# A gate's division by remainder with all its intermediates in SBUF, and its denominator scaled on ScalarE

## Chip, cores and metric

The kernel runs on one core of a Trainium2 chip. The metric is device time in microseconds (us). TensorE (PE) multiplies matrices, VectorE (DVE), ScalarE (ACT) and GpSimd (POOL) work element by element, and SyncE (SP) issues the DMAs. SBUF is the working memory on the core, PSUM holds what PE writes.

## What is computed

Sliding-window attention of 8 batches and 8 heads over 576 positions, and behind it a feed-forward layer of 4608 tokens, 512 to 2048 to 512, whose activation is a rational function:

```python
scores = scale * np.matmul(q, k.transpose(0, 1, 3, 2))     # masked to a window of 64
attn = np.exp(scores - np.max(scores, axis=-1, keepdims=True))
attn = attn / (np.sum(attn, axis=-1, keepdims=True) + 1e-09)
x = np.matmul(attn, v)                                      # heads joined: 4608 x 512
h = x @ w_in
P = a[0] + a[1] * h + a[2] * h**2 + a[3] * h**3
Q = 1.0 + np.abs(b[0]) * np.abs(h) + np.abs(b[1]) * h**2
out = (P / (Q + 1e-6)) @ w_out
```

The weights come as 64-bit floats and are decoded on the chip.

## The kernel before

**Tiling.** The tokens go in 12 chunks of 384 (CH). The inner width of 2048 goes in 16 slices of 128. One *step* is one slice of one chunk: `ffn1` (line 234) makes h, 128 x 384, by 12 matmuls into PSUM and issues the gate; `ffn2` (line 270) multiplies the gate's result with w_out, 9 matmuls into three accumulators of 128 x 512. There are 192 steps. Every matrix operand is split into a high part, rounded to PE's fp32r format, and a low part, the remainder; so each product is three matmuls (high with high, low with high, high with low), and each gate must deliver gh (high) and gl (low).

**Attention.** A chunk has four attention units (two heads each). A unit loads q, k and v, makes scores on PE (S in ps_s, line 182), scales and masks them on DVE (lines 188 and 192), takes the maximum (nmx, line 198), runs six exponentials on ACT that also sum (line 201), adds and inverts the sums on DVE (203, 204), scales on POOL (sm, line 205), transposes on PE (212), copies on ACT (pT, 214), and multiplies with v (223), from which ACT and DVE make xh and xl (228, 229). A unit comes about every four steps.

**Decoding.** `decode` (line 101) loads a slice of 512 columns, makes the 32-bit number in five DVE instructions (lines 113 to 118), rounds it on ACT (121) and subtracts on POOL (122). There are 32 decodes, spread over the first 20 or so steps.

**The gate** (lines 241 to 261), step by step: ACT takes ah = |h| (244) and num = a3 h + a2 (245), both from PSUM; DVE makes num = (num h) and then (num + a1) h (246, 247); POOL makes u = b1 ah + b0 (248) and u = u ah (249), so that Q = u + QADD with QADD = 1 + 1e-6; ACT takes ah = Ln(u + QADD) (251) and ah = Exp(-ah) (252), a first value of 1/Q; DVE refines it by one Newton step, u = (u + QADD) ah and u = (2 - u) ah (253, 254), and makes num = (num + a0) u (255); ACT rounds it to gh (258), and gl = num - gh (260) runs on POOL for the first 20 gates (GLN) and on DVE for the rest.

**Order and buffers.** Every engine takes its instructions in program order and waits at each for what it needs. That order is made by a scheduler at build time, which simulates the engines, so that an edit of the gate can move other instructions too. The tiles ah, u and num have two buffers each (pool tmp), gh and gl four (LAG + 1), h two, each accumulator one. So a step's tiles come free when the second step before it is done with them. `ffn2` of a step is written three steps (LAG) after its `ffn1`.

Of the kernel before, what the change touches and what calls it, by code (L numbers as in the profile page):

```python
# [9 lines left out]
F32 = mybir.dt.float32  # L10
F32R = mybir.dt.float32r
U32 = mybir.dt.uint32
AF = mybir.ActivationFunctionType
ALU = mybir.AluOpType
# [3 lines left out]
CH = 384  # L18
TC = CH // WIN
PR = TC // 2  # L20
GLN = 20
AHEAD = 3
LAG = 3
W_AT = 0, 1, 2, 3
# [3 lines left out]
QADD = 1.0 + 1e-6  # L28
# [3 lines left out]
def swa_rational_ffn(ctx: ExitStack, tc: tile.TileContext, qT, kT, v, w_in, w_out, a, b, out):  # L32
    nc = tc.nc
    P = 128
# [17 lines left out]
    gp = ctx.enter_context(tc.tile_pool(name="gp", bufs=LAG + 1))  # L52
    op = ctx.enter_context(tc.tile_pool(name="op", bufs=2))
# [26 lines left out]
    a_sb = const.tile([P, 4], F32, name="a_sb")  # L80
    b_raw = const.tile([P, 2], F32, name="b_raw")
    b_sb = const.tile([P, 2], F32, name="b_sb")
# [146 lines left out]
        nc.vector.tensor_tensor(out=xl[c, hp], in0=x, in1=xh[c, hp].bitcast(F32), op=ALU.subtract)  # L229

    gs = {}
    n_gates = [0]

    def ffn1(c, i):
        h = ps_h.tile([P, CH], F32, name="h")
        n = 0
        for cc in range(NCC):
            for w, x in ((wi_h, xl), (wi_h, xh), (wi_l, xh)):
                nc.tensor.matmul(h, w[:, cc, i * P:(i + 1) * P], x[c, cc], start=n == 0, stop=n == 3 * NCC - 1)  # L239
                n += 1  # L240
        ah = tmp.tile([P, CH], F32, name="ah")
        u = tmp.tile([P, CH], F32, name="u")
        num = tmp.tile([P, CH], F32, name="num")
        nc.scalar.activation(ah, h, AF.Abs)  # L244
        nc.scalar.activation(num, h, AF.Identity, scale=a_sb[:, 3:4], bias=a_sb[:, 2:3])  # L245
        nc.vector.tensor_tensor(out=num, in0=num, in1=h, op=ALU.mult)
        nc.vector.scalar_tensor_tensor(out=num, in0=num, scalar=a_sb[:, 1:2], in1=h, op0=ALU.add, op1=ALU.mult)  # L247
        nc.gpsimd.tensor_scalar(out=u, in0=ah, scalar1=b_sb[:, 1:2], scalar2=b_sb[:, 0:1], op0=ALU.mult, op1=ALU.add)  # L248
        nc.gpsimd.tensor_tensor(out=u, in0=u, in1=ah, op=ALU.mult)  # L249

        nc.scalar.activation(ah, u, AF.Ln, bias=QADD)  # L251
        nc.scalar.activation(ah, ah, AF.Exp, scale=-1.0)  # L252
        nc.vector.scalar_tensor_tensor(out=u, in0=u, scalar=QADD, in1=ah, op0=ALU.add, op1=ALU.mult)  # L253
        nc.vector.scalar_tensor_tensor(out=u, in0=u, scalar=2.0, in1=ah, op0=ALU.subtract, op1=ALU.mult, reverse0=True)  # L254
        nc.vector.scalar_tensor_tensor(out=num, in0=num, scalar=a_sb[:, 0:1], in1=u, op0=ALU.add, op1=ALU.mult)  # L255
        gh = gp.tile([P, CH], F32R, name="gh")
        gl = gp.tile([P, CH], F32R, name="gl")
        nc.scalar.copy(out=gh, in_=num)  # L258
        n_gates[0] += 1
        (nc.gpsimd if n_gates[0] <= GLN else nc.vector).tensor_tensor(out=gl, in0=num, in1=gh.bitcast(F32), op=ALU.subtract)  # L260
        gs[c, i] = gh, gl


# [83 lines left out]
    for s in range(total + LAG):  # L347
        for fn, *args in todo.get(s, ()):
            if fn in (load_w_in, load_w_out):
                fn(*args)  # L350
        if s < total:
            ffn1(*steps[s])
        for fn, *args in todo.get(s, ()):
            if fn not in (load_w_in, load_w_out):
                fn(*args)
        if s >= LAG:
            ffn2(s - LAG)
# [31 lines left out]
```

## Time and profile before

| | |
|---|---|
| median of 3 runs | 1064.74 us (1063.88 to 1066.21) |
| the profiled execution, its span | 1063.77 us, 1062.0 us |
| PE busy | 963.7 us, 91% of the span, 6624 matmuls |
| DVE busy | 917.7 us, 86%, 1583 instructions |
| ACT busy | 674.3 us, 63%, 1702 |
| POOL busy | 525.0 us, 49%, 511 |

How to read the profile: it is one execution, with times from its start. A group's row gives line, engine, operation, output and inputs, shape, count, then the busy time in us, the mean of one in ns, and the idle time of its engine just before, with what ended it. A row in the order of time begins with its start and its duration. A row of waits says who waited for whom: us in total, times, longest. A row of a stage gives its limits and length, then the busy time and count of PE, its weight load, DVE, ACT and POOL, and then PE's granted clock, the DMA's share and GB/s. A line's own row gives the least, the median and the greatest duration in ns. PE's matmuls overlap, so its busy time is no measure of its throughput. L260 is line 260.

### The profile page before, as it was taken

What the parts mean: (1) busy time and instruction counts of PE and PEld (TensorE: products, weight loads), DVE (VectorE), ACT (ScalarE), POOL (GpSimd) and SP (SyncE); (2) the same over time, 40 slices, a digit from 0 to 9 for tenths busy, and PEclk for the clock granted to TensorE, in tenths of its full rate; (3) what the DMA queues carried; (4) which work ended last, traced back from release to release, by engine and by line L of the source; (5) the groups of instructions that cost most, each with busy time, mean ns of one, the idle gap of its engine ahead of it and who ended that gap; (6) DMA issues with size and microseconds to landing.
All of it is one profiled execution on the core that took longest, in us unless ns stands there. A gap on an engine that the chain in (4) does not pass through costs nothing.

```text
span 1062.0 us, 18218 instructions
## 1 busy us (share of the span) xinstructions
PE 963.7 (91%) x6624; PEld 846.0 (80%) x6624; DVE 917.7 (86%) x1583; ACT 674.3 (63%) x1702; POOL 525.0 (49%) x511
## 2 busy tenths in 40 slices
PE   2558667899999999999999999999999999999997
PEld 2446555778888888888888888888888888888996
DVE  6999989988888898898888888888888888888885
ACT  3454445467666766766766766766666667667654
POOL 5356658864454445435435535534444444454432
PEclk9778779899999999999999999999999999999999
DMA  5543343102121121110211211210211211200000
GB/s 183 173 152 93 107 130 110 35 1 73 48 66 30 59 58 32 63 61 28 70 45 29 69 48 33 92 31 28 85 29 30 88 30 32 93 16 1 31 2 30
DMA packets 68538, 64.10 MB, mean 60 GB/s; under 512 B 4448, under 2 KB 61792, under 8 KB 68448
## 3 DMA queue, kind: packets, MB, share of 16 engines
q1 hardware_dynamic: 68448, 62.93, 19.0%
q8 instruction: 52, 0.85, 0.3%
q14 instruction: 38, 0.31, 0.1%
HBM read 53.48 MB, written 9.44 MB: 59 GB/s over the span
## 4 chain that ended last, share of the span: by engine, by line
DVE 36%; ACT 20%; POOL 19%; PE 17%; issue 5%; DMA 3%; POOLq 0%; SPq 0%; DVEq 0%; ACTq 0%
PE o L280 8%; ACT sm L201 8%; POOL u L248 7%; PE h L239 7%; DVE u L253 7%; POOL u L249 6%; POOL sm L205 4%; DVE u L254 4%; DVE nmx L198 4%; DVE num L255 2%; ACT ah L251 2%; DVE w_c L117 2%; DVE gl L260 2%; ACT ah L252 2%; DVE w_c L118 2%
## 5 line engine op out<-in xcount | busy, mean ns | idle before, releaser
L239 PE MATMUL h<-xl,wi_h 128*128 128x384 f32 x768 | 269.4, 351 | 30.3 <-DVE num L247 22.3
L248 POOL TENSOR_SCALAR u<-ah,b_sb 128x384 f32<-128x384 f32 x192 | 164.6, 860 | 262.8 <-ACT ah L244 199.6
L239 PE MATMUL h<-xh,wi_h 128*128 128x384 f32 x768 | 264.3, 344 | 0.0
L239 PE MATMUL h<-xh,wi_l 128*128 128x384 f32 x768 | 263.5, 343 | 0.0
L280 PE MATMUL o<-wo_h,gl 128*128 128x512 f32 x576 | 236.8, 411 | 25.4 <-DVE gl L260 14.4
L280 PE MATMUL o<-wo_h,gh 128*128 128x512 f32 x576 | 228.6, 397 | 0.0
L280 PE MATMUL o<-wo_l,gh 128*128 128x512 f32 x576 | 228.0, 396 | 0.0
L249 POOL TENSOR_TENSOR u<-u,ah 128x384 f32<-128x384 f32 x192 | 204.5, 1071 | 9.8
L239 PEld LDWEIGHTS h<-xl,wi_h 128*128 128x128 f32 x768 | 148.2, 193 | 40.1 <-DVE num L247 26.1
L205 POOL TENSOR_TENSOR sm<-sm,rs 128x768 f32<-128x768 f32 x48 | 81.4, 1696 | 195.8 <-DVE rs L204 195.8
L201 ACT ACTIVATE sm<-sm,nmx 128x128 f32<-128x128 f32 x288 | 111.9, 390 | 102.7 <-DVE nmx L198 102.4
L260 DVE TENSOR_TENSOR gl<-num,gh 128x384 fp32r<-128x384 f32 x172 | 154.0, 899 | 13.0 <-ACT gh L258 10.0
L245 ACT ACTIVATE num<-h,a_sb 128x384 f32<-128x384 f32 x192 | 128.5, 670 | 45.7 <-DVE gl L260 35.8
L280 PEld LDWEIGHTS o<-wo_h,gl 128*128 128x128 f32 x576 | 109.6, 190 | 58.9 <-DVE gl L260 19.2
L239 PEld LDWEIGHTS h<-xh,wi_h 128*128 128x128 f32 x768 | 148.5, 193 | 4.7
L253 DVE SCALAR_TENSOR_TENSOR u<-u,ah 128x384 f32<-128x384 f32 x192 | 116.7, 608 | 40.9 <-ACT ah L252 39.2
L251 ACT ACTIVATE ah<-u 128x384 f32<-128x384 f32 x192 | 100.4, 523 | 80.2 <-POOL u L249 79.3
L239 PEld LDWEIGHTS h<-xh,wi_l 128*128 128x128 f32 x768 | 148.3, 193 | 0.0
L280 PEld LDWEIGHTS o<-wo_h,gh 128*128 128x128 f32 x576 | 109.7, 190 | 25.2
L258 ACT CAST gh<-num 128x384 fp32r<-128x384 f32 x192 | 96.7, 508 | 47.5 <-DVE num L255 47.4
L280 PEld LDWEIGHTS o<-wo_l,gh 128*128 128x128 f32 x576 | 109.9, 191 | 18.7
L255 DVE SCALAR_TENSOR_TENSOR num<-num,a_sb,u 128x384 f32<-128x384 f32 x192 | 121.1, 636 | 2.9
(45 smaller groups left out, 1274.1 us busy)
## 6 DMA issues: line engine op xcount, KB each, us to landing
out<-ob SPq DMA_DIRECT2D x33, 256.0 KB, 2.0
w_st<-w_in SPq DMA_DIRECT2D x16, 512.0 KB, 3.7
w_st<-w_out SPq DMA_DIRECT2D x16, 512.0 KB, 3.6
q<-qT SPq DMA_DIRECT2D x32, 192.0 KB, 3.4
vt<-v SPq DMA_DIRECT2D x16, 384.0 KB, 3.4
vt<-v SPq DMA_DIRECT2D x16, 320.0 KB, 3.3
kt<-kT SPq DMA_DIRECT2D x16, 224.0 KB, 3.5
kt<-kT SPq DMA_DIRECT2D x16, 192.0 KB, 3.5
```

Of the source, the lines that this page charges most:

```text
L201: nc.scalar.activation(sm[:, j, :], sm[:, j, :], AF.Exp, bias=nmx[:, j:j + 1], accum_out=sums[:, j:j + 1])
L205: nc.gpsimd.tensor_tensor(out=sm, in0=sm, in1=rs.unsqueeze(2).broadcast_to([P, NR, P]), op=ALU.mult)
L239: nc.tensor.matmul(h, w[:, cc, i * P:(i + 1) * P], x[c, cc], start=n == 0, stop=n == 3 * NCC - 1)
L245: nc.scalar.activation(num, h, AF.Identity, scale=a_sb[:, 3:4], bias=a_sb[:, 2:3])
L248: nc.gpsimd.tensor_scalar(out=u, in0=ah, scalar1=b_sb[:, 1:2], scalar2=b_sb[:, 0:1], op0=ALU.mult, op1=ALU.add)
L249: nc.gpsimd.tensor_tensor(out=u, in0=u, in1=ah, op=ALU.mult)
L251: nc.scalar.activation(ah, u, AF.Ln, bias=QADD)
L253: nc.vector.scalar_tensor_tensor(out=u, in0=u, scalar=QADD, in1=ah, op0=ALU.add, op1=ALU.mult)
L255: nc.vector.scalar_tensor_tensor(out=num, in0=num, scalar=a_sb[:, 0:1], in1=u, op0=ALU.add, op1=ALU.mult)
L258: nc.scalar.copy(out=gh, in_=num)
L260: (nc.gpsimd if n_gates[0] <= GLN else nc.vector).tensor_tensor(out=gl, in0=num, in1=gh.bitcast(F32), op=ALU.subtract)
L280: nc.tensor.matmul(acc[c][t], g[:, ts], w[:, i, :], start=first and n == 0, stop=last and n == 2)
```

## The change

The gate divides in another way. The product of num + a0 and the first value of 1/Q is rounded to fp32r as it is written, and that is gh. Then the remainder of the division is formed, num + a0 - (u + QADD) gh, and multiplied with the same value of 1/Q; that is gl. The Newton step, the rounding copy on ACT and the subtraction for gl go. The scaling b1 ah + b0 goes from POOL to ACT. POOL keeps the product u ah, and no gl runs on POOL any more.

```diff
-        nc.gpsimd.tensor_scalar(out=u, in0=ah, scalar1=b_sb[:, 1:2], scalar2=b_sb[:, 0:1], op0=ALU.mult, op1=ALU.add)
+        nc.scalar.activation(u, ah, AF.Identity, scale=b_sb[:, 1:2], bias=b_sb[:, 0:1])
...
         nc.scalar.activation(ah, u, AF.Ln, bias=QADD)
         nc.scalar.activation(ah, ah, AF.Exp, scale=-1.0)
-        nc.vector.scalar_tensor_tensor(out=u, in0=u, scalar=QADD, in1=ah, op0=ALU.add, op1=ALU.mult)
-        nc.vector.scalar_tensor_tensor(out=u, in0=u, scalar=2.0, in1=ah, op0=ALU.subtract, op1=ALU.mult, reverse0=True)
-        nc.vector.scalar_tensor_tensor(out=num, in0=num, scalar=a_sb[:, 0:1], in1=u, op0=ALU.add, op1=ALU.mult)
-        nc.scalar.copy(out=gh, in_=num)
-        n_gates[0] += 1
-        (nc.gpsimd if n_gates[0] <= GLN else nc.vector).tensor_tensor(out=gl, in0=num, in1=gh.bitcast(F32), op=ALU.subtract)
+        nc.vector.scalar_tensor_tensor(out=gh, in0=num, scalar=a_sb[:, 0:1], in1=ah, op0=ALU.add, op1=ALU.mult)
+        nc.vector.scalar_tensor_tensor(out=u, in0=u, scalar=QADD, in1=gh.bitcast(F32), op0=ALU.add, op1=ALU.mult)
+        nc.vector.scalar_tensor_tensor(out=num, in0=num, scalar=a_sb[:, 0:1], in1=u, op0=ALU.add, op1=ALU.subtract)
+        nc.vector.tensor_tensor(out=gl, in0=num, in1=ah, op=ALU.mult)
```

In the changed kernel the lines are: 246 scaling on ACT, 247 and 248 num, 249 the product on POOL, 252 Ln, 253 Exp, 254 gh, 255 and 256 the remainder, 257 gl; the attention's lines are smaller by one, the output's by three.

Where the instructions stand. First ACT around the softmax of one attention unit in the middle of the program, before (each row is an instruction, its output and inputs and their size):

```order
L251 ACTIVATE ah<-u 128x384
L228 CAST xh_5434<-ps_x 128x384
L252 ACTIVATE ah<-ah 128x384
L251 ACTIVATE ah<-u 128x384
L252 ACTIVATE ah<-ah 128x384
L201 ACTIVATE sm,sums<-sm,nmx 128x128 x6
L258 CAST gh<-num 128x384
L244 ACTIVATE ah<-h 128x384
L258 CAST gh<-num 128x384
L245 ACTIVATE num<-h,a_sb 128x384
```

The same place on ACT now:

```order
L252 ACTIVATE ah<-u 128x384
L227 CAST xh_4917<-ps_x 128x384
L253 ACTIVATE ah<-ah 128x384
L252 ACTIVATE ah<-u 128x384
L253 ACTIVATE ah<-ah 128x384
L200 ACTIVATE sm,sums<-sm,nmx 128x128 x6
L244 ACTIVATE ah<-h 128x384
L245 ACTIVATE num<-h,a_sb 128x384
L246 ACTIVATE u<-ah,b_sb 128x384
```

The two copies to gh behind the six exponentials are gone, and each step has the scaling (L246) behind num. In the one unit of four that ends a chunk, one copy of the output (ob) now stands behind the exponentials, and two ahead of them.

Next DVE at the same kind of place, before:

```order
L253 SCALAR_TENSOR_TENSOR u<-u,ah 128x384
L188 SCALAR_TENSOR_TENSOR sm<-ps_s,mask 128x384 x2
L253 SCALAR_TENSOR_TENSOR u<-u,ah 128x384
L254 SCALAR_TENSOR_TENSOR u<-u,ah 128x384
L198 TENSOR_REDUCE nmx<-sm 128x6
L254 SCALAR_TENSOR_TENSOR u<-u,ah 128x384
L255 SCALAR_TENSOR_TENSOR num<-num,a_sb,u 128x384 x2
L203 TENSOR_SCALAR sums<-sums 128x6
L204 RECIPROCAL rs<-sums 128x6
L260 TENSOR_TENSOR gl<-num,gh 128x384 x2
```

And now:

```order
L187 SCALAR_TENSOR_TENSOR sm<-ps_s,mask 128x384 x2
L254 SCALAR_TENSOR_TENSOR gh<-num,a_sb,ah 128x384 x2
L197 TENSOR_REDUCE nmx<-sm 128x6
L255 SCALAR_TENSOR_TENSOR u<-u,gh 128x384 x2
L256 SCALAR_TENSOR_TENSOR num<-num,a_sb,u 128x384 x2
L257 TENSOR_TENSOR gl<-num,ah 128x384 x2
L202 TENSOR_SCALAR sums<-sums 128x6
L203 RECIPROCAL rs<-sums 128x6
```

The two gl have moved ahead of the instruction on the softmax's sums; in some units the second of them stands between it and the reciprocal.

Last POOL in the startup, while weights are decoded, before:

```order
L248 TENSOR_SCALAR u<-ah,b_sb 128x384
L205 TENSOR_TENSOR sm<-sm,rs 128x768
L260 TENSOR_TENSOR gl<-num,gh 128x384 x2
L122 TENSOR_TENSOR wo_l<-w_c,wo_h 128x512
L249 TENSOR_TENSOR u<-u,ah 128x384
L122 TENSOR_TENSOR wo_l<-w_c,wo_h 128x512
L260 TENSOR_TENSOR gl<-num,gh 128x384
L122 TENSOR_TENSOR wo_l<-w_c,wo_h 128x512
L260 TENSOR_TENSOR gl<-num,gh 128x384
L122 TENSOR_TENSOR wo_l<-w_c,wo_h 128x512
```

And now:

```order
L249 TENSOR_TENSOR u<-u,ah 128x384
L121 TENSOR_TENSOR wo_l<-w_c,wo_h 128x512
L249 TENSOR_TENSOR u<-u,ah 128x384
L204 TENSOR_TENSOR sm<-sm,rs 128x768
L121 TENSOR_TENSOR wo_l<-w_c,wo_h 128x512
L121 TENSOR_TENSOR wi_l<-w_c,wi_h 128x4x128
```

L248 and L260 are gone from POOL. On DVE, 17 gl now stand ahead of the last instruction of the last decode, where none stood; there were 16 whole gates ahead of it and now there are 17. PE's order has the same groups, and differs in the startup, at the ends of chunks and at the end, where the products of three steps follow the last h, and before it of four.

More of the change, by code (lines that the diff above doesn't have):

```diff
@@ L20 @@
 PR = TC // 2
-GLN = 20
 AHEAD = 3
@@ L231, in swa_rational_ffn @@
     gs = {}
-    n_gates = [0]
     def ffn1(c, i):
@@ L243, in ffn1 @@
         num = tmp.tile([P, CH], F32, name="num")
+        gh = gp.tile([P, CH], F32R, name="gh")
+        gl = gp.tile([P, CH], F32R, name="gl")
         nc.scalar.activation(ah, h, AF.Abs)
         nc.scalar.activation(num, h, AF.Identity, scale=a_sb[:, 3:4], bias=a_sb[:, 2:3])
+        nc.scalar.activation(u, ah, AF.Identity, scale=b_sb[:, 1:2], bias=b_sb[:, 0:1])
         nc.vector.tensor_tensor(out=num, in0=num, in1=h, op=ALU.mult)
         nc.vector.scalar_tensor_tensor(out=num, in0=num, scalar=a_sb[:, 1:2], in1=h, op0=ALU.add, op1=ALU.mult)
-        nc.gpsimd.tensor_scalar(out=u, in0=ah, scalar1=b_sb[:, 1:2], scalar2=b_sb[:, 0:1], op0=ALU.mult, op1=ALU.add)
         nc.gpsimd.tensor_tensor(out=u, in0=u, in1=ah, op=ALU.mult)
@@ L252, in ffn1 @@
         nc.scalar.activation(ah, ah, AF.Exp, scale=-1.0)
[L253 to L258, printed above, removed]
-        n_gates[0] += 1
-        (nc.gpsimd if n_gates[0] <= GLN else nc.vector).tensor_tensor(out=gl, in0=num, in1=gh.bitcast(F32), op=ALU.subtract)
+        nc.vector.scalar_tensor_tensor(out=gh, in0=num, scalar=a_sb[:, 0:1], in1=ah, op0=ALU.add, op1=ALU.mult)
+        nc.vector.scalar_tensor_tensor(out=u, in0=u, scalar=QADD, in1=gh.bitcast(F32), op0=ALU.add, op1=ALU.mult)
+        nc.vector.scalar_tensor_tensor(out=num, in0=num, scalar=a_sb[:, 0:1], in1=u, op0=ALU.add, op1=ALU.subtract)
+        nc.vector.tensor_tensor(out=gl, in0=num, in1=ah, op=ALU.mult)
         gs[c, i] = gh, gl
```

## The prediction

> **What bounds the kernel now.** I read the page's slices first, then the stages, then who waits for whom in each. The slices (each digit tenths of a slice of 26.6 us):
>
> ```profile
> PE   2558667899999999999999999999999999999997
> DVE  6999989988888898898888888888888888888885
> ```
>
> TensorE (PE) is filled only from the eighth slice on; before that VectorE (DVE) is the full engine. The busy times by stage (microseconds; columns PE, weight load, DVE, ACT, POOL) put figures to it:
>
> ```profile
> 58.00:205.00 147.00, 100.53 (x609) 83.97 (x608) 139.46 (x219) 73.86 (x188) 101.18 (x77) 0.81 0.35 106
> 300.00:940.00 640.00, 628.28 (x4474) 557.82 (x4473) 551.39 (x979) 442.80 (x1138) 299.84 (x294) 1.00 0.16 49
> ```
>
> So there are two regimes. From 58 to 205 us the weights are decoded while the first gates run: DVE is busy 139.5 of 147 us, PE idles 46.5, and a microsecond less on DVE is about one less in the end. From 300 to 940 us PE idles only 640 - 628.3 = 11.7 us, and only that can be won. The waits of PE in that stretch have a single row, and its largest part looks like this in the order of time (start, duration, what, idle before):
>
> ```profile
> PE o L280 <- DVE gl L260: 11.7, 9, 1.6
> ...
> 456.80 0.40 ACT L201 ACTIVATE sm<-sm,nmx 128x128 f32<-128x128 f32 x1 [2.77 <-DVE nmx L198]
> ...
> 459.50 0.91 ACT L258 CAST gh<-num 128x384 fp32r<-128x384 f32 x2
> ...
> 457.15 1.14 DVE L255 SCALAR_TENSOR_TENSOR num<-num,a_sb,u 128x384 f32<-128x384 f32 x2
> ...
> 460.03 2.48 DVE L260 TENSOR_TENSOR gl<-num,gh 128x384 fp32r<-128x384 f32 x2 [0.38 <-ACT gh L258]
> ...
> 459.11 0.33 PE L239 MATMUL h<-xh,wi_l 128*128 128x384 f32 x1
> 460.82 0.50 PE L280 MATMUL o<-wo_h,gl 128*128 128x512 f32 x1 [1.38 <-DVE gl L260]
> ```
>
> The gate's values num are complete at 457.15 + 1.14 = 458.3, but their rounded copy gh stands on ACT behind six softmax exponentials that wait for nmx, so gl starts at 460.03 and PE loses 1.38 us.
>
> **The change, steady stage.** gh is now written by DVE itself from num and the exponential, and gl follows two DVE instructions later; no step of the gate after Exp leaves DVE, and in the new order both gl stand ahead of the softmax sums that DVE awaits from ACT, or one of them does. Counted with the durations above, the four instructions take the place of u, u, num, gl one for one, so the first gl would end near 458.3 + 0.55 = 458.9, ahead of the 459.4 at which PE's last h matmul ends. What is late next is the front of the chain. The scaling u, now on ACT, waits behind num instead of running on POOL beside it. No row shows this instruction; the nearest are
>
> ```profile
> L251 ACT ACTIVATE ah<-u 128x384 f32<-128x384 f32 x192 | 100.4, 523 | 80.2 <-POOL u L249 79.3
> ...
> L245 ACT ACTIVATE num<-h,a_sb 128x384 f32<-128x384 f32 x192 | 128.5, 670 | 45.7 <-DVE gl L260 35.8
> ...
> L258 ACT CAST gh<-num 128x384 fp32r<-128x384 f32 x192 | 96.7, 508 | 47.5 <-DVE num L255 47.4
> ...
> L248 POOL TENSOR_SCALAR u<-ah,b_sb x192: 654/688/2607, 58.5 to 1048.2; 128x384 f32<-128x384 f32 x192
> ...
> 338.66 2.44 ACT sm L201 x12
> 357.83 2.44 ACT sm L201 x12
> ```
>
> (The last row but two gives the least, the median and the most in ns; the last two are the softmax of two attention units in the chain that ended last.) The two ends are 0.52 us (SBUF source, no scale operand) and 0.67 us (two operands per partition, PSUM source). I take 0.70, since it has both the operands and the SBUF source. ACT gains 0.70 and loses 0.51 a step, 0.19 x 130 steps = 25 us in the 640, so 468 of 640 us: not a bound. The chain to Exp gets longer by about num's 0.57 (start to start) plus 0.70 less POOL's 0.69, 0.6 us, and shorter behind it by the copy's 0.51 and by the wait for ACT. Laid out for one attention unit (four steps, 357.83 - 338.66 = 19.2 us) with these durations I find the first gl of the unit about 1.3 us ahead of PE's need; before it is 0.35 us ahead in an ordinary unit:
>
> ```profile
> 439.21 0.56 DVE L260 TENSOR_TENSOR gl<-num,gh 128x384 fp32r<-128x384 f32 x1
> ...
> 440.12 0.39 PE L280 MATMUL o<-wo_h,gl 128*128 128x512 f32 x1
> ```
>
> (439.77 against PE's turn to it at 440.12). One wait is added: ah is now read until gl, so Abs of step s waits for gl of step s-2; behind it in ACT's queue stand num, the scaling, Ln and Exp of the step, and POOL and DVE wait for those. Before, num waited for that same gl, so Abs alone moves, by some 0.4 us. gh's buffer is asked for earlier too, but there are four of them and the second product of step s-4 precedes the end of h of step s in PE's order. So all nine waits go: **-11.7 us**; the ends are -11.7 and, if each only moves to another instruction, 0.
>
> **The change, startup.** Here DVE is the bound, and it shares something with POOL. A stretch without POOL's work beside it gives the bare durations, the groups of the stage (us busy, mean ns) the real ones:
>
> ```profile
> 90.09 0.55 DVE L253 SCALAR_TENSOR_TENSOR u<-u,ah 128x384 f32<-128x384 f32 x1
> 90.56 0.41 DVE L113 TENSOR_SCALAR w_c<-w_st 128x512 uint32<-128x512 uint32 x1
> 90.90 0.68 DVE L117 SCALAR_TENSOR_TENSOR w_c<-w_st,w_c 128x512 uint32<-128x512 uint32 x1
> ...
> 92.91 0.60 DVE L255 SCALAR_TENSOR_TENSOR num<-num,a_sb,u 128x384 f32<-128x384 f32 x1
> ...
> L118 DVE SCALAR_TENSOR_TENSOR w_c<-w_st,w_c 128x512 uint32<-128x512 uint32 x31 | 31.9, 1034 | 0.1
> L117 DVE SCALAR_TENSOR_TENSOR w_c<-w_st,w_c 128x512 uint32<-128x512 uint32 x32 | 30.6, 959 | 0.3
> L114 DVE TENSOR_SCALAR w_c<-w_c 128x512 f32<-128x512 f32 x32 | 20.8, 648 | 0.3
> L116 DVE TENSOR_SCALAR w_c<-w_c 128x512 uint32<-128x512 uint32 x32 | 19.9, 621 | 0.3
> L113 DVE TENSOR_SCALAR w_c<-w_st 128x512 uint32<-128x512 uint32 x32 | 18.4, 574 | 16.7 <-DMA w_st<-w_in 12.7 <-DMA w_st<-w_out 1.5 <-POOL wo_l L122 1.4
> L253 DVE SCALAR_TENSOR_TENSOR u<-u,ah 128x384 f32<-128x384 f32 x16 | 14.2, 888 | 0.0
> L254 DVE SCALAR_TENSOR_TENSOR u<-u,ah 128x384 f32<-128x384 f32 x16 | 13.1, 830 | 0.0
> L255 DVE SCALAR_TENSOR_TENSOR num<-num,a_sb,u 128x384 f32<-128x384 f32 x16 | 11.5, 730 | 0.0
> ```
>
> Excess over bare (0.68 for L117 and L118, 0.41 for L113, L114, L116, 0.55 for L253 and L254, 0.60 for L255): 10.8 + 8.8 + 7.7 + 6.8 + 5.3 + 5.4 + 4.3 + 1.9 = 51 us that DVE lost up to 205 us. POOL's groups in the same window:
>
> ```profile
> L122 POOL TENSOR_TENSOR wi_l<-w_c,wi_h 128x512 fp32r<-128x512 f32 x16 | 23.4, 1462 | 23.6 <-ACT wi_h L121 23.6
> L248 POOL TENSOR_SCALAR u<-ah,b_sb 128x384 f32<-128x384 f32 x17 | 22.0, 1293 | 10.7 <-DVE num L255 5.4 <-ACT wi_h L121 3.7 <-ACT ah L244 1.7
> L122 POOL TENSOR_TENSOR wo_l<-w_c,wo_h 128x512 fp32r<-128x512 f32 x15 | 21.1, 1409 | 18.9 <-ACT wo_h L121 12.4 <-DVE rs L204 6.5
> L249 POOL TENSOR_TENSOR u<-u,ah 128x384 f32<-128x384 f32 x17 | 20.4, 1201 | 0.7
> L260 POOL TENSOR_TENSOR gl<-num,gh 128x384 fp32r<-128x384 f32 x15 | 19.4, 1298 | 10.3 <-ACT gh L258 10.3
> L205 POOL TENSOR_TENSOR sm<-sm,rs 128x768 f32<-128x768 f32 x10 | 16.1, 1610 | 11.8 <-DVE rs L204 11.8
> ```
>
> Together 122.4 us, so 51/122.4 = 0.42 us of DVE's loss for each. The change takes L260's 19.4 away, 8.1 us of loss. L248's 22.0 us are mostly its own waiting, since its quiet length is 0.654: 17 x 0.654 = 11.1, worth 4.7. Relief: 12.8 us, between 0 and the 41.4 that both are busy. Against it, 17 gl now stand on DVE ahead of the last decode: 17 x 0.55 = 9.4 bare (a gl on DVE has its quickest at 0.548), and each meets POOL as L253 to L255 do: (14.2 + 13.1 + 11.5)/48 = 0.81 less a bare 0.57, 0.24 x 17 = 4.1. Price 13.5, between 9.4 and 17 x 0.899 = 15.3, the mean of gl over the run:
>
> ```profile
> L260 DVE TENSOR_TENSOR gl<-num,gh 128x384 fp32r<-128x384 f32 x172 | 154.0, 899 | 13.0 <-ACT gh L258 10.0
> L260 DVE TENSOR_TENSOR gl<-num,gh x172: 548/562/1822, 232.2 to 1054.0; 128x384 fp32r<-128x384 f32 x172
> ```
>
> Net **+0.7 us**, ends 9.4 - 41.4 = -32 and +15.3. I take the middle because both prices come from rows of the same stage. The Trainium skill (VectorE: DVE Perf Modes, The TRN2 errata) gives a two-input fp32 instruction (N + 151)/0.96 ns, an estimate of 557 ns for 384 elements. The quickest gl agrees, the mean of 899 does not; by the page the price would be 9.5 and the net -3.3 us.
>
> **The tail.** PE's last stretch waited 2.2 us for gl:
>
> ```profile
> L280 PE MATMUL o<-wo_h,gl 128*128 128x512 f32 x60 | 23.9, 398 | 2.2 <-DVE gl L260 2.2
> ```
>
> The chain behind the last h loses a copy (0.51) and gains the scaling's 0.6; **0**, give or take 1.5.
>
> **Sum.** The profiled execution took 1063.77 us (span 1062.0 and 1.8 around it); -11.7 + 0.7 + 0 = -11.0 gives 1052.8. It lies 0.97 us under the median of the runs, so on their scale 1064.74 - 11.0 = **1053.7 us**. A measurement can tell about 0.2% here, 2.1 us.
>
> **Rivals.** *POOL's absence frees DVE in full.* If every microsecond of the removed POOL work had held DVE, the startup nets 41.4 - 13.5 = 28 us and the time is 1064.7 - 11.7 - 28 = 1025. For: DVE's excesses reach twice the bare length. Against: DVE lost 51 us beside 122 of POOL, not 122. The Trainium skill (SBUF — State Buffer, SBUF: two separate sides) has the shared ports as an exclusive lock, held for the whole instruction by whichever engine came first; the 2.48 us for two gl beside POOL's work agree, but DVE instructions that read PSUM would still pass. Chance 0.07.
>
> *No relief in the startup.* Decode and softmax on POOL catch DVE as often as before, gl costs 15.3 and the steady win of 11.7 is eaten: 1064.7 + 15.3 - 11.7 = 1068, or about even with half the relief. For: L122 and L249 are 65 of the 122 us and stay. Against: L260 alone ran beside a full DVE. Chance 0.14, about half within 0.2%, half above.
>
> *The gate's loop becomes the pace (slower).* Abs of step s waits for gl of step s-2, and two steps must fit into 9.6 us of PE. If the longer front and the softmax between pairs cost each unit more than the 1.0 to 1.3 us of margin that I count, PE waits in every unit: at 0.5 us beyond it, 40 units x 0.5 = 20 us, 1064.7 - 11.7 + 0.7 + 20 = 1074. For: the margin before was 0.35 us. Against: gl no longer waits behind ACT, and POOL's instruction beside it is gone. Chance 0.13.
>
> *The waits only move* to the copies of the output that stand round the six exponentials in ACT's queue once a chunk: 1064.7 + 0.7 = 1065, same. Chance 0.06.
>
> **How the numbers follow.** The forecast has 0.60. Faster: 0.60 + 0.07, and 0.04 of the cases with half the relief, 0.71; same: 0.06 and 0.05, 0.11; slower: 0.13 and 0.05, 0.18. The range runs from 1041 (12 us of extra relief, between forecast and first rival) to 1067 (no relief); it leaves out most of the loop's rival and of the first, 0.2 in all.
>
> **What would show it.** Right: PE's idle time from 300 to 940 us under 3 us; no wait of PE for gl there; DVE's busy share in that stretch falling from 86% to near 79%, as gl drops from 0.90 to about 0.56 us; the last decode on DVE still near 205 us; u on ACT near 0.70 us. Wrong: PE waiting for gl or num once in every unit of 19 us (the loop), or the last decode later than 215 us (no relief) or earlier than 195 (full relief).

## The result and the profile after

The changed kernel takes 1040.59 us, the median of four runs (1040.2 to 1041.14), beside 1065.47 of the kernel before (1063.88 to 1066.47): a ratio of 0.977, 95% interval 0.975 to 0.979. The profiled execution took 1040.44 us with a span of 1038.7, so it is 23.3 us shorter than the one shown of before. The forecast was 1053.7, with a range down to 1041: the direction was right, but more than twice the forecast gain came, and the time lies 0.4 us below the lower end of the range.

The page after, busy times, two rows of slices (26 us each) and two groups of the gate:

```profile
PE 955.6 (92%) x6624; PEld 844.3 (81%) x6624; DVE 863.1 (83%) x1603; ACT 706.8 (68%) x1702; POOL 323.5 (31%) x299
...
PE   2567667889999999999999999999999999999997
...
DVE  6999989988887888888877877887888888878776
...
L249 POOL TENSOR_TENSOR u<-u,ah 128x384 f32<-128x384 f32 x192 | 198.6, 1035 | 391.7 <-ACT u L246 354.9
...
L246 ACT ACTIVATE u<-ah,b_sb 128x384 f32<-128x384 f32 x192 | 135.4, 708 | 0.0
```

POOL lost 200 us of work, DVE is full only while weights are decoded (142.5 of 147 us in the first stage below), and the scaling takes 0.708 us on ACT, where 0.70 was taken. The stages after, and below them the ramp before, which the prediction doesn't show (columns as in the table of stages there: PE, weight load, DVE, ACT, POOL, granted clock):

```profile
58.00:205.00 147.00, 105.57 (x663) 89.56 (x664) 142.48 (x247) 80.70 (x207) 62.85 (x46) 0.86 0.36 110
205.00:318.58 113.58, 109.74 (x722) 96.08 (x721) 96.46 (x175) 77.49 (x180) 34.40 (x30) 0.98 0.14 44
300.00:940.00 640.00, 640.00 (x4638) 571.71 (x4637) 520.47 (x1007) 480.32 (x1162) 183.62 (x167) 1.00 0.16 50
```

```profile
205.00:327.85 122.85, 119.69 (x783) 103.45 (x781) 106.60 (x180) 80.20 (x199) 63.27 (x62) 1.00 0.14 44
```

From 300 to 940 us PE now has no idle time at all; before it had 11.7 us. To see where the 23.3 us went, take PE's clock time at equal points of the program: the first h matmul of step 42 (the third chunk is under way) and of step 138 (six chunks on), and the last matmul. Before:

```profile
327.85 0.42 PE L239 MATMUL h<-xl,wi_h 128*128 128x384 f32 x1
...
798.88 0.42 PE L239 MATMUL h<-xl,wi_h 128*128 128x384 f32 x1
...
1057.95 0.40 PE L280 MATMUL o<-wo_h,gh 128*128 128x512 f32 x1
```

After, with the last wait of the tail ahead of the last row:

```profile
318.58 0.34 PE L237 MATMUL h<-xl,wi_h 128*128 128x384 f32 x1
...
777.87 0.34 PE L237 MATMUL h<-xl,wi_h 128*128 128x384 f32 x1
...
1032.67 0.51 PE L277 MATMUL o<-wo_h,gl 128*128 128x512 f32 x1 [2.27 <-DVE gl L257]
...
1034.63 0.40 PE L277 MATMUL o<-wo_h,gh 128*128 128x512 f32 x1
```

Step 42 comes 9.3 us earlier, and a chunk takes (798.88 - 327.85)/6 = 78.5 us before and 76.55 after. But PE's order is another: at step 42 PE has 1641 matmuls behind it after, and 1651 before. At an equal count of matmuls (the 1652nd, with which step 42 begins before) the lead is 7.8 us; in the 300 matmuls around it the lead swings between 6.8 and 10.9 and is 8.3 on average. Near the end it is the same. Up to the h of step 190, before and after:

```profile
0.00:1043.22 1043.22, 950.83 (x6564) 835.34 (x6565) 908.05 (x1567) 666.39 (x1687) 521.60 (x507) 0.97 0.20 61
```

```profile
0.00:1017.66 1017.66, 940.49 (x6555) 831.99 (x6556) 851.88 (x1584) 697.08 (x1684) 320.40 (x296) 0.97 0.20 62
```

The lead is 25.6 us there, but with 9 matmuls fewer behind it; at an equal count (the 6565th) it is 24.0, and at the last matmul 23.3. So the startup brings some 8 us, the steady part some 16, and the tail gives less than 1 back. The terms were forecast at +0.7, -11.7 and 0.

### The profile page after: what moved, and what is told of

Read it like the earlier page. It is cut to its first block, busy times and chain, and to the rows that moved or that the text cites. A ratio compares the mean times of both kernels' runs of the same rounds, so it can differ in the third digit from the quotient of the medians.

```text
span 1038.7 us, 18237 instructions
## 1 busy us (share of the span) xinstructions
PE 955.6 (92%) x6624; PEld 844.3 (81%) x6624; DVE 863.1 (83%) x1603; ACT 706.8 (68%) x1702; POOL 323.5 (31%) x299
## 4 chain that ended last, share of the span: by engine, by line
PE 78%; DVE 16%; issue 2%; DMA 1%; ACT 1%; POOL 0%; SPq 0%; POOLq 0%; DVEq 0%
PE o L277 35%; PE h L237 34%; PE ps_x L222 3%; PE ps_s L181 3%; PE ps_s L211 2%; DVE w_c L116 2%; DVE gh L254 2%; DVE w_c L113 2%; DVE w_c L117 2%; DVE w_c L112 1%; DVE w_c L115 1%; DMA w_st<-w_in 1%; DVE u L255 1%; DVE num L256 1%; DVE gl L257 1%
## 5 line engine op out<-in xcount | busy, mean ns | idle before, releaser
L249 POOL TENSOR_TENSOR u<-u,ah 128x384 f32<-128x384 f32 x192 | 198.6, 1035 | 391.7 <-ACT u L246 354.9
L277 PE MATMUL o<-wo_h,gl 128*128 128x512 f32 x576 | 234.2, 407 | 20.7 <-DVE gl L257 20.7
L247 DVE TENSOR_TENSOR num<-num,h 128x384 f32<-128x384 f32 x192 | 106.2, 553 | 105.7 <-ACT num L245 105.0
L244 ACT ACTIVATE ah<-h 128x384 f32<-128x384 f32 x192 | 94.4, 491 | 142.7 <-PE h L237 81.6
L204 POOL TENSOR_TENSOR sm<-sm,rs 128x768 f32<-128x768 f32 x48 | 73.4, 1529 | 251.1 <-DVE rs L203 244.2
L254 DVE SCALAR_TENSOR_TENSOR gh<-num,a_sb,ah 128x384 fp32r<-128x384 f32 x192 | 124.1, 657 | 25.9 <-ACT ah L253 25.9
L246 ACT ACTIVATE u<-ah,b_sb 128x384 f32<-128x384 f32 x192 | 135.4, 708 | 0.0
L248 DVE SCALAR_TENSOR_TENSOR num<-num,a_sb,h 128x384 f32<-128x384 f32 x192 | 117.8, 613 | 5.8
L256 DVE SCALAR_TENSOR_TENSOR num<-num,a_sb,u 128x384 f32<-128x384 f32 x192 | 119.4, 637 | 0.6
```

The lines of the kernel that those rows point to most:

```text
L204: nc.gpsimd.tensor_tensor(out=sm, in0=sm, in1=rs.unsqueeze(2).broadcast_to([P, NR, P]), op=ALU.mult)
L246: nc.scalar.activation(u, ah, AF.Identity, scale=b_sb[:, 1:2], bias=b_sb[:, 0:1])
L254: nc.vector.scalar_tensor_tensor(out=gh, in0=num, scalar=a_sb[:, 0:1], in1=ah, op0=ALU.add, op1=ALU.mult)
L277: nc.tensor.matmul(acc[c][t], g[:, ts], w[:, i, :], start=first and n == 0, stop=last and n == 2)
```

## The experiments

For the startup there were two theories. One, theory A in the expectations: DVE's loss to POOL's work was priced too low, and taking that work away is the whole of the startup's gain. The rival: the prediction's prices are right, and the gain comes from the shorter chain of the gate or from the new order. For the steady part: the wait behind the copy on ACT alone, as predicted (theory B), against a share of POOL's scaling in the chain, against the buffers of num. All the kernels compute the whole function; where one has work that nothing reads, its heading says so. "Step 42" is how much earlier than before the first h matmul of step 42 starts, "equal count" how much earlier the 1652nd matmul starts, and "a chunk" is the mean of the six chunks from step 42. The scheduler makes a new order for every edit. In 2, 8, 9 and 11 PE has as many matmuls behind it at step 42 as before, within one, and the two leads agree. In the changed kernel and in the others it has more or fewer, and a lead is good to 2 or 3 us there; in 1, 3, 4, 6 and 7 a chunk isn't regular either.

| kernel | median us | ratio, 95% | step 42, us | equal count, us | a chunk, us |
|---|---|---|---|---|---|
| before, in the runs beside these | 1064.6 to 1065.9 | 1 | 0 | 0 | 78.5 |
| changed | 1040.59 | 0.975 to 0.979 | 9.3 | 7.8 | 76.55 |
| 1. before, scaling on ACT | 1057.64 | 0.991 to 0.995 | 3.1 | 4.7 | 78.0 |
| 2. before, all gl on DVE | 1062.01 | 0.996 to 0.998 | 2.3 | 2.3 | 78.5 |
| 3. both of these | 1052.88 | 0.987 to 0.990 | 11.6 | 10.2 | 78.7 |
| 4. changed, scaling on POOL | 1055.48 | 0.989 to 0.993 | 6.9 | 6.0 | 78.0 |
| 5. changed, idle work on POOL | 1048.06 | 0.982 to 0.985 | 7.6 | 6.7 | 77.1 |
| 6. changed, a copy in the chain | 1116.82 | 1.047 to 1.050 | 4.0 | 10.3 | 85.5 |
| 7. before, third buffer for num | 1071.38 | 1.004 to 1.008 | 3.4 | 2.1 | 80.1 |
| 8. changed, early softmax scaling on ACT | 1031.49 | 0.966 to 0.970 | 19.5 | 19.5 | 76.85 |
| 9. changed, first 20 gl on POOL | 1049.06 | 0.983 to 0.986 | 2.8 | 2.8 | 76.85 |
| 10. changed, idle copy on ACT | 1044.65 | 0.978 to 0.983 | 9.0 | 7.5 | 76.85 |
| 11. before, early softmax scaling on ACT | 1055.94 | 0.989 to 0.993 | 9.5 | 9.5 | 78.5 |

**1 to 3: the moves alone, with the Newton step kept.** In 1 the scaling goes to ACT, in 2 the gl of the first 20 gates to DVE, in 3 both; so 3 has the work of POOL that the changed kernel has, and the old division.

```diff
-        nc.gpsimd.tensor_scalar(out=u, in0=ah, scalar1=b_sb[:, 1:2], scalar2=b_sb[:, 0:1], op0=ALU.mult, op1=ALU.add)
+        nc.scalar.activation(u, ah, AF.Identity, scale=b_sb[:, 1:2], bias=b_sb[:, 0:1])
```

```diff
-GLN = 20
+GLN = 0
```

> The kernel before with one part of the change: the scaling b1 ah + b0 on ACT, the Newton step and the copy to gh kept. Theory A (the startup gain is GpSimd work taken out of VectorE's way): the startup ends 5 to 9 us earlier, for L248's share of VectorE's loss was put at 4.7 and at most 9.3. Theory B (the steady gain comes from the copy to gh leaving ACT): PE's waits for gl, 11.7 us from 300 to 940 us, stay or grow. Together 1056 to 1061 us. Rival (the scaling's place does not matter): 1065 us within 2.

> The kernel before with every gl on VectorE (GLN 0), nothing else. By the prediction's prices the startup loses 13.5 us of VectorE and wins 8.1: 1070 us. Rival (a gl on GpSimd held VectorE for its whole time, 19.4 us in the startup): 1065 + 13.5 - 19.4 = 1059 us. The steady waits for gl stay in both.

> The kernel before with the scaling on ACT and every gl on VectorE, so that GpSimd has the work of the changed kernel, but the Newton step and the copy to gh stay. Theory A: the startup is as in the changed kernel, 9 us ahead of before at step 42; theory B: the waits for gl in the steady stage stay, so 1056 us. Rival (the remainder formula is what brings the startup gain, by a shorter chain or another order): no gain at step 42, 1065 us.

The totals up to step 42, of before, 2 and 3 (the columns are those of the stages: PE, weight load, DVE, ACT, POOL):

```profile
0.00:327.85 327.85, 246.51 (x1651) 208.74 (x1651) 293.67 (x476) 175.48 (x454) 190.80 (x178) 0.89 0.31 95
```

```profile
0.00:325.53 325.53, 243.40 (x1650) 209.17 (x1651) 294.67 (x496) 176.45 (x455) 164.15 (x158) 0.88 0.31 96
```

```profile
0.00:316.21 316.21, 239.45 (x1641) 203.50 (x1642) 288.32 (x493) 197.90 (x492) 132.45 (x115) 0.91 0.32 98
```

In 2, DVE has 20 instructions more, 11 us at 0.55, and is busy only 1.0 us longer: the 26.7 us less on POOL gave back 10. Besides, DVE idles 3.3 us less, 30.9 us for 34.2, and that makes the lead. By the prediction's prices this move cost 9.4 + 4.1 - 8.1 = 5.4 us, and 1070 us were expected; it gained 2.3. In 1 the gain of 3.1 to 4.7 is near the 4.7 that was priced. In 3, POOL works 58.4 us less, and the startup gains as much as in the changed kernel (at step 36 it is 9.2 us in both), though the division is the old one; 3 took 1052.9 us, where 1056 were expected. So the two moves are enough for the startup's gain. At an equal count 1 and 2 bring 7.0 us together, for 7.8 in the changed kernel and 10.2 in 3; with the swing of the order that doesn't tell whether the moves add up or help each other. Nor is the new division without effect: 4 has it and the gl on DVE, but the scaling on POOL, and gains 6.0, which is 3.7 more than 2.

In the steady stretch the moves give next to nothing. In 3, PE still waits 4.7 us for gl from 300 to 940 us, and a chunk is no shorter. The waits of PE from 300 to 940 us in 1:

```profile
PE o L280 <- DVE gl L260: 4.0, 5, 0.9
```

Two thirds of the 11.7 us of waiting for gl are gone there with the copy still on ACT, where they were expected to stay, yet a chunk is only 0.5 us shorter.

**4: the changed kernel with the scaling back on POOL.**

```diff
-        nc.scalar.activation(u, ah, AF.Identity, scale=b_sb[:, 1:2], bias=b_sb[:, 0:1])
...
+        nc.gpsimd.tensor_scalar(out=u, in0=ah, scalar1=b_sb[:, 1:2], scalar2=b_sb[:, 0:1], op0=ALU.mult, op1=ALU.add)
```

> The changed kernel with the scaling back on GpSimd: the remainder formula alone. Theory B: PE's waits for gl in the steady stage are gone, worth 14 us; theory A: of the startup's 9 us some 4 stay (gl is off GpSimd, the scaling is not). 1047 us, with 1045 to 1051 as the range. Rival to B (the steady gain is GpSimd's scaling no longer colliding with gl on VectorE): the waits stay, 1060 us.

PE's waits from 300 to 940 us:

```profile
PE h L237 <- DVE num L247: 3.9, 6, 0.9
PE ps_x L222 <- ACT pT L213: 3.4, 6, 0.7
PE o L277 <- DVE gl L257: 0.7, 4, 0.2
```

The new division takes the waits for gl away, as predicted, but with the scaling on POOL others come in their place, and a chunk takes 78.0 us; so 4 took 1055.5 us, where 1045 to 1051 were expected. Neither half of the change gives the steady gain: 0.5 us a chunk with either, 1.95 with both.

**5 and 10: the load without the chain.** In 5 POOL does the old scaling into a tile w that nothing reads, in 10 ACT copies gh into one.

```diff
+        w = tmp.tile([P, CH], F32, name="w")
...
+        nc.gpsimd.tensor_scalar(out=w, in0=ah, scalar1=b_sb[:, 1:2], scalar2=b_sb[:, 0:1], op0=ALU.mult, op1=ALU.add)
```

```diff
+        w = tmp.tile([P, CH], F32, name="w")
...
+        nc.scalar.copy(out=w, in_=gh.bitcast(F32))
```

> The changed kernel with one more instruction on GpSimd in each step: the scaling again, from ah into a tile that nobody reads, so that GpSimd is as loaded as with its own scaling but the gate's chain does not run through it. Theory A (contention): VectorE's excess in the startup grows by about 7 us, as the scaling on ACT took 7 us from it: 1048 us from that alone. Theory D (the steady gain needs GpSimd light as well as the copy gone): the time of a chunk goes from 76.55 us to about 78, nine chunks, 13 us more, together 1058 to 1061 us. Rival to D (the remainder formula with the scaling on GpSimd lost its steady gain because the chain ran through GpSimd): chunks stay at 76.6 and the time is 1048 us.

> The changed kernel with one more copy on ACT in each step, gh into a tile that nobody reads: ACT has a copy as before and it waits in ACT's queue for VectorE, but the gate's chain does not run through it. PE's order in the steady stage stays that of the changed kernel. If the copy's place in the chain made the steady waits, the chunks stay at 76.6 us and the time at 1041 to 1043 us. Rival (ACT's queue held up by an instruction that waits for VectorE is enough): chunks of 78 us, 1052 us or more.

The stretch from 300 to 940 us in 10, and PE's waits there in 5:

```profile
300.00:940.00 640.00, 640.00 (x4625) 570.99 (x4624) 519.16 (x1003) 535.69 (x1290) 183.60 (x167) 1.00 0.16 50
```

```profile
PE o L279 <- ACT ob L293: 1.9, 1, 1.9
PE o L279 <- DVE gl L259: 0.4, 2, 0.2
```

With 536 us of 640 on ACT PE still waits for nothing, in nearly the same order of steps, and a chunk is 0.3 us longer; 10 took 1044.65 us, 2 more than expected. That isn't the copy's price, since 8 and 9 have the same 76.85 with nothing added to the changed gate's steady part. POOL's load off the chain costs 0.54 us a chunk against the changed kernel and 0.24 against 8 to 10, of the 1.95 in all; only 2.3 us of it shows as waits. So the load of the scaling on POOL is a small part of what it costs the steady stage. That its place in the chain makes the rest is argued from 4, whose order is another too.

The startup of 5, up to step 42:

```profile
0.00:320.23 320.23, 241.16 (x1644) 204.84 (x1645) 287.81 (x497) 182.15 (x456) 166.03 (x158) 0.93 0.32 97
```

POOL works 43.3 us more than in the changed kernel (122.76 us, shown with 8 and 11 below) and DVE, with as many instructions, is busy 1.9 us more, 287.81 for 285.87. Theory A expected 7 us there. That 5 took the 1048 us it named is luck: 1.7 us are lost by step 42, and the rest comes in the steady part and the tail.

**6: the copy back in the chain.** The quotient goes to a plain tile, and ACT copies it to gh.

```diff
-        nc.vector.scalar_tensor_tensor(out=gh, in0=num, scalar=a_sb[:, 0:1], in1=ah, op0=ALU.add, op1=ALU.mult)
+        nc.vector.scalar_tensor_tensor(out=w, in0=num, scalar=a_sb[:, 0:1], in1=ah, op0=ALU.add, op1=ALU.mult)
+        nc.scalar.copy(out=gh, in_=w)
```

> The changed kernel with a copy on ACT put back into the chain: VectorE writes the quotient to a plain tile, ACT rounds it to gh, and the remainder goes on from gh. GpSimd's work is that of the changed kernel. Theory B (the copy behind the softmax on ACT makes the steady waits): chunks go back to 78 us or more, nine of them, so 1053 to 1058 us, with waits of PE for gl; the startup keeps its 9 us. Rival (GpSimd's load alone makes the waits): 1041 to 1045 us.

```profile
PE o L279 <- DVE gl L259: 29.8, 30, 1.1
PE ps_s L211 <- POOL sm L204: 5.4, 19, 0.5
```

A chunk takes 9 us more, PE waits for gl 30 times in the stretch, and the time is some 60 us above what was expected. The same copy off the chain cost 0.3 us at most, so it is the copy's place between two steps of DVE that costs. Its size isn't clean, since this remainder needs gh on DVE twice and the scheduler laid out another order around it.

**7: a third buffer for num in the kernel before.**

```diff
-        num = tmp.tile([P, CH], F32, name="num")
+        num = tmp.tile([P, CH], F32, name="num", bufs=3)
```

> The kernel before with a third buffer for num, so that num of a step does not wait for gl of the second step before it. If the loop through two buffers makes the steady waits: PE's 11.7 us of waits for gl fall by half or more, 1055 to 1060 us. Theory B (the copy stands behind the exponentials whatever the buffers): the waits stay, 1064 us within 2.

It got slower, by 0.4 to 0.8%, where 1055 to 1060 or 1064 us were expected. 7.6 us of waiting for gl are left in the stretch, a third less and not the half, and 6.2 us of other waits come beside them. So a third buffer for num doesn't bring the gain; what part the two buffers have in the old waits isn't settled, since the order is a new one.

**8, 9, 11: POOL's other work in the startup.** 8 and 11 leave the gate as it is, in the changed kernel and in the one before, and take the softmax scaling of the first ten attention units from POOL to ACT. 9 puts the gl of the changed kernel's first 20 gates on POOL.

```diff
-        nc.gpsimd.tensor_tensor(out=sm, in0=sm, in1=rs.unsqueeze(2).broadcast_to([P, NR, P]), op=ALU.mult)
+        if c < 2 or (c == 2 and hp < 2):
+            for j in range(NR):
+                nc.scalar.activation(sm[:, j, :], sm[:, j, :], AF.Identity, scale=rs[:, j:j + 1])
+        else:
+            nc.gpsimd.tensor_tensor(out=sm, in0=sm, in1=rs.unsqueeze(2).broadcast_to([P, NR, P]), op=ALU.mult)
```

```diff
-        nc.vector.tensor_tensor(out=gl, in0=num, in1=ah, op=ALU.mult)
+        n_gates[0] += 1
+        (nc.gpsimd if n_gates[0] <= 20 else nc.vector).tensor_tensor(out=gl, in0=num, in1=ah, op=ALU.mult)
```

> The changed kernel with the softmax's scaling in the first ten attention units on ACT (six instructions with one factor per row) in place of GpSimd. It takes about 19 us of GpSimd's work out of the startup. Theory A, at the 0.4 to 0.6 us of VectorE's time that each microsecond of gl or scaling on GpSimd had cost: 8 to 11 us faster, 1030 to 1033 us. Rival (six short instructions on ACT delay the gates and the transposes by as much): 1040 us or more.

> The changed kernel with gl of the first 20 gates back on GpSimd, the rest on VectorE. Theory A: gl on VectorE costs it 0.55 us bare and saves it more than that in waiting for GpSimd, so the startup gets longer: at step 36 some 4 us (the nine of the change less the five of the remainder alone, or of the scaling alone), 1044 to 1046 us. Rival (the prediction's prices, by which the move of gl costs 5 us): 1035 us. The steady stage keeps its 76.6 us a chunk in both.

> The kernel before with the softmax's scaling in the first ten attention units on ACT in place of GpSimd: VectorE keeps every instruction it had, so that only what GpSimd takes from it changes. Theory A: 16 us of GpSimd's work leave the startup, at 0.5 us of VectorE's time each 8 us earlier at step 36, 1056 to 1059 us. Rival (VectorE's excess is not GpSimd's doing, and the scheduler's other order brought the nine us): 1065 us within 2.

The totals up to step 42 in 11, then those of the changed kernel, then those of 8:

```profile
0.00:318.40 318.40, 239.90 (x1650) 205.62 (x1651) 280.23 (x476) 193.51 (x514) 173.00 (x168) 0.91 0.31 98
```

```profile
0.00:318.58 318.58, 241.40 (x1641) 206.50 (x1642) 285.87 (x497) 179.63 (x454) 122.76 (x115) 0.89 0.32 98
```

```profile
0.00:308.40 308.40, 235.21 (x1651) 200.21 (x1651) 271.93 (x500) 201.41 (x518) 107.10 (x106) 0.93 0.33 101
```

11 is the cleanest test of the theory: DVE has the same 476 instructions as before, POOL works 17.8 us less, DVE is busy 13.4 us less, and step 42 comes 9.5 us earlier, with not a line of the gate changed and the steady part unmoved. On the changed kernel (8) the same edit takes 15.7 us from POOL and 13.9 from DVE (which does three instructions more), and gives another 10 to 12 us. It makes the fastest kernel here, 1031.49 us. 9 loses 5.0 us of the startup's gain at an equal count (2.8 for 7.8), where some 4 were expected and a gain by the prediction's prices; its chunk is the 76.85 of 8 and 10, and so it takes 1049 us, 3 more than expected. The first product of ffn2 from 58 to 205 us, there:

```profile
L279 PE MATMUL o<-wo_h,gl 128*128 128x512 f32 x42 | 23.9, 568 | 24.1 <-POOL gl L259 24.1
```

and in the changed kernel:

```profile
L277 PE MATMUL o<-wo_h,gl 128*128 128x512 f32 x48 | 22.8, 476 | 16.0 <-DVE gl L257 16.0
```

PE waits 8 us more for a gl on POOL than for one on DVE. At the equal count DVE is busy 1.6 us longer in 9, with 19 instructions fewer, and idles 3.4 us more. So in 9 the place of gl in the chain can count beside the load. 11 and 8 show the load alone, since nothing of the gate moves there: the rival by which DVE's excess isn't POOL's doing falls. But they price the softmax scaling, at 0.75 and 0.89 us of DVE for each of POOL, and not the work that the change moved. For that 2 gives 10 of 26.7, or 0.37, and 5 gives 1.9 of 43.3, no more than the 0.42 of the prediction. So that DVE's loss to this work was priced too low isn't shown.

## Why the prediction was off, step by step

**Steady, -11.7: the mechanism right, the size short, the cause half.** PE waits no more for gl between 300 and 940 us, nor for anything else. The term was to be between 0 and -11.7, as more idle time there wasn't. Yet 640 us hold 8.15 chunks of 78.5, and 1.95 us less in each is 16 us. The missing 4 us were in PE's busy time: in the six chunks from step 42, with the same 3312 matmuls, PE idles 8.2 us before and none after, and is busy 462.9 us before and 459.3 after. Half of these 3.6 us is missing in 8, 9 and 10 (461.1 us, no idle time), which have the changed gate too; why PE's busy time got shorter stays open. And the copy on ACT was only half the cause. The prediction had the scaling's move as a small cost of the chain, 0.70 for 0.69; 4 shows that with the scaling on POOL the steady gain is 0.5 us a chunk, as it is in 1 with the old division and its copy on ACT. ACT's load was no bound, as said (480 us for the predicted 468, and 536 in 10 did little). DVE's share fell from 86% to 81%, for the 79% said.

**Startup, +0.7: this step failed.** The groups of DVE up to 205 us after, to be held against those of before in the prediction:

```profile
L116 DVE SCALAR_TENSOR_TENSOR w_c<-w_st,w_c 128x512 uint32<-128x512 uint32 x31 | 28.0, 904 | 0.3
L117 DVE SCALAR_TENSOR_TENSOR w_c<-w_st,w_c 128x512 uint32<-128x512 uint32 x31 | 23.7, 763 | 0.1
L113 DVE TENSOR_SCALAR w_c<-w_c 128x512 f32<-128x512 f32 x31 | 19.4, 625 | 0.2
L112 DVE TENSOR_SCALAR w_c<-w_st 128x512 uint32<-128x512 uint32 x32 | 17.6, 550 | 13.8 <-DMA w_st<-w_in 8.8 <-POOL wi_l L121 3.3 <-POOL wo_l L121 1.4
L254 DVE SCALAR_TENSOR_TENSOR gh<-num,a_sb,ah 128x384 fp32r<-128x384 f32 x17 | 16.8, 993 | 0.5 <-ACT ah L253 0.5
L115 DVE TENSOR_SCALAR w_c<-w_c 128x512 uint32<-128x512 uint32 x31 | 16.4, 529 | 0.3
L256 DVE SCALAR_TENSOR_TENSOR num<-num,a_sb,u 128x384 f32<-128x384 f32 x17 | 13.9, 822 | 0.0
L255 DVE SCALAR_TENSOR_TENSOR u<-u,gh 128x384 f32<-128x384 f32 x17 | 12.1, 716 | 0.2
L257 DVE TENSOR_TENSOR gl<-num,ah 128x384 fp32r<-128x384 f32 x17 | 12.0, 711 | 0.0
```

With the prediction's bare durations (0.60 for L254 and L256, 0.55 for L255 and L257) the excess is 24.4 us in the decode and 15.7 in the gate, 40.1 in all. Up to there the two sizes were near: 17 gl, 9.4 us bare, with 2.7 of own waiting for the 4.1 said, and an excess of 40.1, where 51 - 12.8 + 4.1 = 42.3 were to be left. And DVE's idle time up to 205 us, which had no term, fell by 2.4. The totals to there, before:

```profile
0.00:205.00 205.00, 126.82 (x870) 105.29 (x871) 187.06 (x297) 95.28 (x256) 127.53 (x117) 0.83 0.41 126
```

and after:

```profile
0.00:205.00 205.00, 131.66 (x921) 110.42 (x922) 189.41 (x323) 102.14 (x275) 88.36 (x86) 0.84 0.42 127
```

That makes 9.4 - 10.9 - 2.4 = -3.9 us, where +0.7 stood. By 205 us PE has 51 matmuls more behind it (921 from the start, 870 before), and in the ramp, where it is busy 97% of the time in both kernels, 61 fewer ahead, worth 61 x 0.152 = 9.3 us; the ten between the two are the order's, 1.5 us. Counted on DVE over the whole way to step 42, with the totals shown, the 9.3 are its own: it is busy 7.8 us less (293.7 to 285.9) though it does 21 instructions more, and idles 1.5 us less (34.2 to 32.7).

The experiments put the error at a place. At an equal count the scaling alone, priced at -4.7 us, gave -4.7 (1; -3.1 at step 42). The gl alone was priced at +5.4 and gave -2.3 (2), and moved back it lost 5.0 (9). So the term that failed is the move of gl, by some 8 us, and that is what the startup was off by, within the swing of the order. In 2 two things were wrong with it. To step 42 the prediction's rates give 20 x (0.55 + 0.24) - 0.42 x 26.7 = 4.6 us more on DVE, and 1.0 was measured. And DVE's idle time, which the sum put at nothing, fell by 3.3 us. What made DVE wait less, the shorter way from num to gl or POOL's being free for the rest, isn't told apart.

PE's granted clock may have a part in it, as it differs in this stage, 0.81 before and 0.86 after. Rows of the same form from 58 to 205 us, before and after:

```profile
L239 PE MATMUL h<-xh,wi_l 128*128 128x384 f32 x64 | 25.9, 404 | 0.0
```

```profile
L237 PE MATMUL h<-xh,wi_l 128*128 128x384 f32 x73 | 27.6, 378 | 0.0
```

Over all forms a matmul took 100.53/609 = 0.165 us and now 0.159, on 663 of them 3.9 us. That is the most that the clock can have given, for PE still idles 41 of the 147 us; no run tests it by itself.

**The tail, 0: right.** PE waits for the last gl 2.27 us, 2.2 before, as said. From an equal count of matmuls to the end 0.7 us are lost (24.0 to 23.3), inside the 1.5 given.

**The signs named beforehand.** Idle time of PE under 3 us, no wait for gl, u near 0.70: these came. The last decode ended near 210 us, within the 195 to 215 given, and so it told nothing: one more gate is done on DVE by 205 us (17 for 16), and the decode ends no earlier (207.5 us before).

**The rivals.** The gate's loop didn't become the pace, the waits didn't move to the output's copies, and the startup had relief. The first rival's full price, 1 us of DVE for each us of POOL, is wrong for the gl (10 of 26.7 in 2) and for the scaling (1.9 of 43.3 in 5), but near for the softmax scaling: 13.4 of 17.8 in 11.

## What to carry to other kernels

Work on GpSimd is priced by what it makes VectorE wait in the stage in which VectorE is full, and the price differs from instruction to instruction: move one and measure it, even when the bottleneck gets more work of its own by it, and look at VectorE's idle time beside its busy time. Compare two traces by the time at equal counts of work done, not by idle time alone, because here the busy time changed too, and not at one named step alone, because a new order shifted that by 2 us. A change with two halves that each give little can give much together, so undo each half before the gain is put down to one cause.

## What the runs showed of the hardware

GpSimd's work slows some VectorE instructions and not others. Up to step 42, before, a decode instruction with two inputs in SBUF and a mask of the scores with one input in PSUM:

```profile
L118 DVE SCALAR_TENSOR_TENSOR w_c<-w_st,w_c 128x512 uint32<-128x512 uint32 x32 | 33.0, 1035 | 0.1
...
L192 DVE SCALAR_TENSOR_TENSOR sm<-ps_s,mask 128x384 f32<-128x384 f32 x22 | 11.1, 547 | 0.0
```

and in 11, with ten softmax scalings less on POOL:

```profile
L118 DVE SCALAR_TENSOR_TENSOR w_c<-w_st,w_c 128x512 uint32<-128x512 uint32 x32 | 28.0, 877 | 0.1
...
L192 DVE SCALAR_TENSOR_TENSOR sm<-ps_s,mask 128x384 f32<-128x384 f32 x22 | 11.1, 548 | 0.0
```

L118 gets 158 ns shorter, L192 stays. The Trainium skill (SBUF — State Buffer, SBUF: two separate sides) says that VectorE and GpSimd share a pair of ports as an exclusive lock, held for a whole instruction, and that on VectorE's side it takes an instruction with two inputs in SBUF or one in a two-port mode. The two rows agree with it. If the lock is the cause, 11 gives it a price in this place: 13.4 us of VectorE for 17.8 us of GpSimd. It isn't one price: the scaling on GpSimd in 5 took 1.9 us of VectorE for 43.3.

TensorE's granted clock differs in the startup. From 58 to 205 us it was 0.81 before, 0.86 after, and in 8:

```profile
58.00:205.00 147.00, 105.92 (x689) 88.15 (x682) 141.75 (x256) 97.55 (x252) 57.53 (x43) 0.90 0.35 106
...
L241 PE MATMUL h<-xh,wi_l 128*128 128x384 f32 x75 | 27.4, 365 | 0.0
```

The same matmul took 404, 378 and 365 ns in the three, and PE was busy 100.5, 105.6 and 105.9 us, so the busier PE had the higher clock. In the first 58 us it went the other way (0.85 before, 0.79 after), and there the clock differs from 0.79 to 0.97 among these kernels, with PE busy for 25 to 27 us in all of them. So this is no rule from these runs. Nor was a microsecond less on VectorE worth more than one: 13.4 us in 11 brought step 42 9.5 us ahead.
